# Attention units of a fused attention, ELU and SiLU kernel: normalising p by a diagonal product on TensorE

## The chip, the cores and the metric

One core of a Trainium2 chip runs the program. The metric is the device time of one execution in microseconds; before the change it is 877.9 us in the median of three runs (876.8 to 879.29).

## The reference

Causal attention with a window of 128 tokens and a linear bias for each head, over 4 sequences of 576 tokens, 8 heads of 64; then two pairs of dense layers, the first with an ELU, the second with a SiLU, on 2304 rows (512 to 2048 to 512 columns each).

```python
scores = scale * np.matmul(q, k.transpose(0, 1, 3, 2))
scores = np.where((rel >= 0) & (rel < 128), scores + bias[None], -1e9)
attn = np.exp(scores - np.max(scores, axis=-1, keepdims=True))
attn = attn / (np.sum(attn, axis=-1, keepdims=True) + 1e-09)
x = heads_to_columns(np.matmul(attn, v))          # 2304 x 512
h = x @ w_in; x = np.where(h > 0, h, np.exp(np.minimum(h, 0)) - 1) @ w_out
h = x @ w2_in; out = (h / (1 + np.exp(-h))) @ w2_out
```

The function that brings the heads into columns is written out in the reference. The weights come as 64-bit floats and are turned into 32-bit ones on the chip.

## The kernel before

**Attention** runs in 36 units. A unit is 256 query tokens of two heads (`UNITS`, L154): two blocks `e` of 128 tokens, two heads `j`. For each unit:

- `scores` (L460): 16 products on 64x64 parts of TensorE write two PSUM tiles `s0`, `s1`, one for each head (L470). VectorE adds the bias, takes the row minimum of the negated scores and writes p (L481); ScalarE takes the exponential in place and adds up the rows into `sm` (L489).
- `normal` (L496): VectorE adds 1e-9 to the four sums of a row and takes reciprocals (L501, L502: 128x4). GpSimd multiplies p by them row by row, four operations (L508).
- `turn` (L511): TensorE transposes p against an identity, 16 transposes of 64 columns (12 where a sequence begins, as in the first four units; L527), into the tile `t` of two banks. The index `x` (upper or lower 64 rows of p) picks the bank. VectorE copies head 0 (L537) and ScalarE head 1 (L539) to `pt` in SBUF, each from both banks.
- `mix` (L543), once for two units: p times v (L559), then to `xt` (L565).

There are three buffers of p and of pt. Two of the bias tables are made by GpSimd with a part masked at the sequence bounds, in `make_cuts` (L447): a copy of 128x1536 bf16 and a memset for each.

**Beside it** the weights are fetched and decoded: GpSimd scales the upper words (L331), ScalarE converts the lower (L333), VectorE joins them (L334, L336), and each weight is split into a high and a low part (L308, L311). The first 4 of 16 column groups of the first layer pair run during attention, block by block of 256 or 512 rows: `split_x` (L573, L574), `hidden` (L600; the ELU by L609, L585, L586, L612, L613) and `output_first` (L627). `make_ahead` forms combinations of blocks of x and stores them. **Then** `layers` runs the rest of both pairs (L927 for the input products, L1018 for the output products).

**The order of the work** is written by a planner (`Plan`, L35). Every piece is added with its engine, an assumed cost, the keys that it reads and writes, and for some a due time. `run` (L72) works backwards to a latest time for each, and then plays the engines forward: an engine that is free takes the ready piece with the earliest latest time. What comes out is each engine's fixed order; the waits on the chip come from the data. Loads go through the SP queue (one early load through ACT's) in the planner's order, over one modelled wire. The due time of a unit's scores is `unit_due` (L457): 4 us plus 3.2 us for each of the first 14 units, then 5.0.

Of the kernel before, what the change touches and what calls it, by code (L numbers as in the profile page):

```python
# [34 lines left out]
class Plan:  # L35
# [11 lines left out]
    def add(self, eng, cost, fn, r=(), w=(), due=1.0e9, moved=0, after=(), floor=0.0):  # L47
# [24 lines left out]
    def run(self):  # L72
        for op in reversed(self.ops):
            op.late = min([op.due] + [b.late - op.cost - self.between(op, b) for b in op.before])
        waiting = {op: len(op.after) for op in self.ops}
        ready = [(0.0, op) for op in self.ops if not op.after]
        queues, free = {}, {}
        for at, op in ready:
            queues.setdefault(op.eng, []).append((at, op))
        now, port = 0.0, 0.0  # L80
        left = len(self.ops)
        while left:
            ran = True
            while ran:
                ran = False
                for eng in queues:
                    if eng and free.get(eng, 0.0) > now:
                        continue
                    can = [x for x in queues[eng] if max(x[0], x[1].floor) <= now]
                    if not can:  # L90
                        continue
                    x = min(can, key=lambda x: (x[1].late, x[1].n))
# [12 lines left out]
                    left -= 1  # L105
                    ran = True
                    end = now + op.cost
                    free[eng] = end
                    if op.moved:
                        port = max(port, now + self.DMA_START) + op.moved / self.DMA_RATE  # L110
                        end = port
# [7 lines left out]
            times = [max(x[0], x[1].floor, free.get(e, 0.0) if e else 0.0) for e, q in queues.items() for x in q]  # L119
            if left:  # L120
                now = min(t for t in times if t > now)
        return max(op.end for op in self.ops)
# [3 lines left out]
def attention_elu_silu_kernel(  # L126
# [49 lines left out]
    UNIT, FAST, NFAST, START = 5.0, 3.2, 14, 4.0  # L176

# [222 lines left out]
    def start():  # L400
        load_q(0, nc.scalar, 1)
        load_k(0, n=1)
        add("DVE", 0.06, lambda: nc.vector.memset(T["warm",], 0.0), w=[("warm",)])
        add("ACT", 1.5, lambda: nc.scalar.activation(T["warm",], T["warm",], AF.Exp), w=[("warm",)], due=0.0)
        add("DVE", 0.27, lambda: nc.vector.memset(T["k", 0][:, :, P // 2:P], 0.0), w=[("kz",)], due=0.0)
        load_k(1, n=1)
        load_q(1, n=1)
        for i in range(3):
            add("DVE", 0.27, lambda i=i: nc.vector.memset(T["p", i][:, :, :, 0:PAD], 0.0), w=[("p", i, "lo")], due=0.1)
            add("DVE", 0.27, lambda i=i: nc.vector.memset(T["p", i][:, :, :, PAD + WIDE:], 0.0), w=[("p", i, "hi")], due=0.1)  # L410
# [12 lines left out]
        for x in range(2):  # L423
            add("POOL", 1.15, lambda x=x: relative(x), w=[("rel",)] + rk, due=0.0)
# [6 lines left out]
        for h in range(H):  # L431
            by = -(2.0 ** (-8.0 * (h + 1) / H)) / scale
            bf, bb = T["biasf",][:, h, P // 2:], T["bias",][:, h, :]
            if h < 2:
# [3 lines left out]
                    r=[("rel",)] + rk, w=[("bias", h)])  # L438
# [7 lines left out]

    def make_cuts():  # L447
        every = [("bias", h) for h in range(H)]

        def cut(name, rows, cols):  # L450
            nc.gpsimd.tensor_copy(T[name,], T["bias",])
            nc.gpsimd.memset(T[name,][rows, :, cols], MASKED / scale)
        add("POOL", 2.9, lambda: cut("biasm", slice(P // 2, P), slice(0, P)), r=every, w=[("biasm", h) for h in range(H)])
        add("POOL", 2.1, lambda: cut("biasa", slice(0, P // 2), slice(0, P // 2)), r=every, w=[("biasa", h) for h in range(H)])
# [5 lines left out]
    def scores(u):  # L460
        t, hp = UNITS[u]

        def products():
            for e in range(2):
                c0 = first_col(2 * t + e) // 2
                for x in range(2):
                    o = e * P + x * (P // 2)
                    for j in range(2):
                        rows = slice(j * D, (j + 1) * D)
                        nc.tensor.matmul(T["s", j][x * (P // 2):(x + 1) * (P // 2), e, c0:], T["q", t % 2][rows, hp, o:o + P // 2],  # L470
                                         T["k", t % 2][rows, hp, o + c0:o + WIDE], start=True, stop=True)
        tensor(0.74, products, r=[("q", t % 2, hp), ("k", t % 2, hp), ("kz",)], w=[("s", 0), ("s", 1)], due=unit_due(u))
        exps = []
        for j in range(2):
            for e in range(2):
# [4 lines left out]
                def biased(j=j, e=e, i=i, c0=c0, b=b):  # L480
                    nc.vector.tensor_tensor_reduce(  # L481
                        T["p", u % 3][:, j, e, PAD + c0:PAD + WIDE], T["s", j][:, e, c0:], T[b,][:, 2 * hp + j, c0:], -scale, 3.0e38,
                        ALU.add, ALU.min, T["neg", u % 4][:, i:i + 1])
                pk = [("p", u % 3, j, e)] + ([("p", u % 3, "lo"), ("p", u % 3, "hi")] if u < 3 else [])
                add("DVE", 0.29, biased, r=[("s", j), (b, 2 * hp + j)], w=pk[:1] + [("neg", u % 4, i)])
# [9 lines left out]

    def normal(u):  # L496
# [6 lines left out]
        add("DVE", 0.3, invert, w=sm)  # L503
        for j in range(2):
# [6 lines left out]
    def turn(u):  # L511
# [8 lines left out]
        def transposes():  # L520
            for j in range(2):
                for a, b2 in parts:
                    for i in range(a, b2):
                        e, c = i // 2, i % 2 * P + PAD
                        for x in range(2):
                            half = slice(x * (P // 2), (x + 1) * (P // 2))
                            nc.tensor.transpose(T["t",][:, x, j, i, :], T["p", u % 3][half, j, e, c - x * PAD:c - x * PAD + P],  # L527
                                                T["ident",][half, half])
        tensor(0.68, transposes, r=[("p", u % 3, j, e) for j in range(2) for e in range(2)]
               + [("p", u % 3, "lo"), ("p", u % 3, "hi"), ("ident",)], w=[("t", 0)], due=unit_due(u + 2) + 0.1)  # L530

        def evict(j):
            for a, b2 in parts:
                dst = T["pt", u % PTS][:, j, a * P:b2 * P].rearrange("p (i x q) -> p i x q", x=2, q=P // 2)
                src = T["t",][:, :, j, a:b2, :].rearrange("p x i q -> p x i q" if False else "p x i q -> p i x q")
                if j == 0:
# [3 lines left out]
        add("DVE", 0.61, lambda: evict(0), r=[("t", 0)], w=[("pt", u % PTS, 0)])  # L540
        add("ACT", 0.5, lambda: evict(1), r=[("t", 0)], w=[("pt", u % PTS, 1)])
# [42 lines left out]
    def elu(src, e):  # L584
        nc.vector.tensor_scalar(e, e, 1.0, -1.0, op0=ALU.min, op1=ALU.add)  # L585
        nc.vector.tensor_tensor(e, src, e, op=ALU.max)  # L586
# [3 lines left out]
    def hidden(bi, f, due):  # L590
# [19 lines left out]
        add("DVE", 0.16 + w * 1.55e-3, lambda: elu(T[m][:, 0:w], T[ek][:, 0:w]), r=[m], w=[ek])  # L610
# [271 lines left out]
    def activated(k, f, half, src, sk):  # L882
# [10 lines left out]
        elif slot("below", 2):  # L893
            def bent():
# [4 lines left out]
                r=[sk], w=[ek])  # L899
            add("ACT", 0.43, lambda: nc.scalar.activation(T[gk[0]], T[ek], AF.Copy), r=[ek], w=[gk[0]])  # L900
        else:
            add("ACT", 0.42, lambda: nc.scalar.activation(T[ek], src(), AF.Exp), r=[sk], w=[ek])
            add("DVE", 0.76, lambda: elu(src(), T[ek]), r=[sk], w=[ek])
# [3 lines left out]
    def quad(k, q, last):  # L907
# [30 lines left out]
        def sum_of(name, src):  # L938
            s, m = K[name], K[src]
            add("DVE", 0.475, lambda: nc.vector.tensor_tensor(T[s], T[m][:, 0:HALF], T[s], op=ALU.add), r=[m], w=[s])  # L940
# [38 lines left out]
    def outputs(k):  # L979
# [6 lines left out]
        for j in range(size):  # L986
            half = j // (size // 2)
            parts = 2 if k == len(steps) - 1 and j == size - 1 else 1
            for part in range(parts):
# [5 lines left out]
                def piece(fp, st=st, w=w, s=s, jj=jj, half=half):  # L995
# [35 lines left out]
                    else:  # L1031
                        add("DVE", 0.08 + w / 960.0, lambda: nc.vector.tensor_tensor(dst, T[m][:, 0:w], dst, op=ALU.add),  # L1032
                            r=[m], w=dk)
# [101 lines left out]
```

## Time and profile before

| | |
|---|---|
| median of three runs | 877.9 us |
| the profiled execution | 878.51 us |
| its span, first to last instruction | 876.7 us |
| TensorE busy | 858.5 us, 98% |
| VectorE, ScalarE, GpSimd busy | 603.1, 507.0, 136.2 us |
| mean granted TensorE clock | 0.994 |

The profile is taken in one execution. PE is TensorE, PEld its weight loads, DVE VectorE, ACT ScalarE, POOL GpSimd. Busy times are shares of the whole span, so a stage that is a twelfth of it hardly shows in them; it is read from tables of its own stretch. An engine's idle time is put down to the event that came last before it went on.

### The profile page before, as it was taken

The numbers are of one execution on the slowest core, as the hardware profiler recorded it, in microseconds if no ns is written. First come the engines' busy times: TensorE is split into PE (matmuls) and PEld (weight loads), VectorE is DVE, ScalarE is ACT, GpSimd is POOL, SyncE is SP. The second block draws the span as 40 slices with busy tenths as digits, with TensorE's granted clock in tenths as the row PEclk, the third lists the DMA queues.
The fourth block names the chain that finished last, engine by engine and source line by source line (L and its number), as shares of the span: only waits on it lengthen the run. The fifth ranks groups of instructions, "written<-read, shape, count | busy, mean of one in ns | idle before, by whom it ended". The sixth has DMA issues, their size and how long they took to land.

```text
span 876.7 us, 15017 instructions
## 1 busy us (share of the span) xinstructions
PE 858.5 (98%) x5520; PEld 772.8 (88%) x5520; DVE 603.1 (69%) x1385; ACT 507.0 (58%) x1191; POOL 136.2 (16%) x238
## 2 busy tenths in 40 slices
PE   6889999999999999999999999999999999999998
PEld 3667777778999999999999998989898989989997
DVE  6988989875997869796869878445746334633333
ACT  6979888865855556563657475656563334533331
POOL 8844434320110001110000220001100000100000
PEclk9979999999999999999999999999999999999999
DMA  9835686459460112280847345142236060226721
GB/s 308 290 116 189 206 270 212 156 188 369 186 243 1 37 55 90 76 322 1 322 170 286 146 150 222 63 189 73 97 113 259 0 252 25 73 73 220 261 97 72
DMA packets 67929, 142.00 MB, mean 162 GB/s; under 512 B 4368, under 2 KB 50192, under 8 KB 67856
## 3 DMA queue, kind: packets, MB, share of 16 engines
q1 hardware_dynamic: 67712, 140.92, 45.3%
q8 instruction: 43, 0.70, 0.3%
q14 instruction: 30, 0.25, 0.1%
q10 hardware_dynamic: 144, 0.13, 0.0%
HBM read 104.07 MB, written 36.96 MB: 161 GB/s over the span
## 4 chain that ended last, share of the span: by engine, by line
PE 89%; DVE 7%; ACT 2%; DMA 1%; issue 1%; POOL 0%; SPq 0%; POOLq 0%; DVEq 0%; ACTq 0%
PE m L1018 37%; PE m L927 33%; PE m L600 5%; PE m L627 5%; PE a L559 3%; PE s L470 3%; PE t L527 2%; DVE raw L334 1%; DVE p L481 1%; DVE raw L336 1%; DVE pt L537 1%; ACT p L489 1%; DVE w L311 1%; DVE g L905 0%; DMA q<-in_q_dram 0%
## 5 line engine op out<-in xcount | busy, mean ns | idle before, releaser
L1018 PE MATMUL m<-w,g 128*128 128x512 f32 (+1 forms) x876 | 211.9, 387 | 0.0
L1018 PEld LDWEIGHTS m<-w,g 128*128 128x128 f32 x876 | 161.6, 188 | 26.2
L1018 PE MATMUL m<-g,w 128*128 128x384 f32 x864 | 162.1, 336 | 0.7 <-DVE e L898 0.7
L1018 PEld LDWEIGHTS m<-g,w 128*128 128x128 f32 x864 | 151.6, 188 | 1.5 <-DVE e L898 1.2
L331 POOL TENSOR_SCALAR raw<-raw 128x512 f32<-128x512 f32 x60 | 47.5, 792 | 539.3 <-DMA raw<-in_moe_w_in_dram 258.3
L905 DVE TENSOR_TENSOR g<-e,g 128x384 fp32r<-128x384 f32 x168 | 93.9, 570 | 49.3 <-ACT e L891 43.1
L940 DVE TENSOR_TENSOR hs<-m,hs 128x384 f32<-128x384 f32 x84 | 46.7, 556 | 85.3 <-PE m L927 84.2
L927 PE MATMUL m<-c,wd 128*128 128x384 f32 x504 | 101.3, 335 | 0.0
L927 PE MATMUL m<-c,wc 128*128 128x384 f32 x504 | 101.2, 335 | 0.0
L927 PE MATMUL m<-c,wa 128*128 128x384 f32 x504 | 98.9, 336 | 0.0
L927 PEld LDWEIGHTS m<-c,wa 128*128 128x128 f32 x504 | 89.2, 188 | 2.6
L927 PEld LDWEIGHTS m<-c,wc 128*128 128x128 f32 x504 | 89.2, 188 | 2.1
L927 PEld LDWEIGHTS m<-c,wd 128*128 128x128 f32 x504 | 89.1, 188 | 2.0
L1032 DVE TENSOR_TENSOR acc<-m,acc 128x384 f32<-128x384 f32 (+2 forms) x85 | 51.4, 607 | 56.8 <-PE m L1018 56.6
L936 ACT ACTIVATE hs<-m 128x384 f32<-128x384 f32 x84 | 41.3, 491 | 84.3 <-PE m L927 83.8
L508 POOL TENSOR_SCALAR p<-p,sm 128x192 f32<-128x192 f32 (+1 forms) x144 | 74.5, 534 | 83.8 <-DVE sm L502 37.9
L489 ACT ACTIVATE p<-p,neg 128x192 f32<-128x192 f32 (+1 forms) x144 | 62.9, 441 | 7.6 <-DVE neg L481 6.6
L627 PE MATMUL m<-g,w 128*128 128x512 f32 (+1 forms) x240 | 57.2, 388 | 1.3 <-DVE e L586 0.7
L892 ACT ACTIVATE g<-hs 128x384 fp32r<-128x384 f32 x48 | 25.3, 527 | 57.2 <-DVE hs L940 56.9
L600 PE MATMUL m<-x,w 128*128 128x512 f32 (+1 forms) x240 | 55.3, 377 | 1.2 <-DVE x L574 1.2
L627 PEld LDWEIGHTS m<-g,w 128*128 128x128 f32 x240 | 42.9, 198 | 11.4 <-issue 1.3
L927 PE MATMUL m<-c,wb 128*128 128x384 f32 x252 | 50.7, 335 | 0.0
(124 smaller groups left out, 1189.2 us busy)
## 6 DMA issues: line engine op xcount, KB each, us to landing
c<-d SPq DMA_DIRECT2D x63, 768.0 KB, 6.6
raw<-in_moe_w_in_dram SPq DMA_DIRECT2D x32, 512.0 KB, 6.2
raw<-in_moe_w_out_dram SPq DMA_DIRECT2D x28, 512.0 KB, 3.6
d<-c SPq DMA_DIRECT2D x14, 768.0 KB, 4.6
d<-st SPq DMA_DIRECT2D x19, 384.0 KB, 3.1
k<-in_k_dram SPq DMA_DIRECT2D x16, 384.0 KB, 5.0
d<-xs SPq DMA_DIRECT2D x14, 384.0 KB, 3.0
v<-in_v_dram SPq DMA_DIRECT2D x18, 256.0 KB, 3.5
```

What stands on the lines that cost most here:

```text
L331: add("POOL", 0.66, lambda: nc.gpsimd.tensor_scalar(f32(top()), f32(top()), 2.0 ** -112, 1.0, op0=ALU.mult, op1=ALU.mult), w=top_k)
L470: nc.tensor.matmul(T["s", j][x * (P // 2):(x + 1) * (P // 2), e, c0:], T["q", t % 2][rows, hp, o:o + P // 2], T["k", t % 2][rows, hp, o + ...
L489: nc.scalar.activation(dst, dst, AF.Exp, bias=T["neg", u % 4][:, i:i + 1], scale=-1.0, accum_out=T["sm", u % 4][:, e, j:j + 1])
L508: nc.gpsimd.tensor_scalar(dst, dst, T["sm", u % 4][:, e, j:j + 1], 1.0, op0=ALU.mult, op1=ALU.mult)
L600: nc.tensor.matmul(T[m][:, 0:w], a[:, cs], T["x0", b2][:, c, 0:w], start=(c == 0 and x == 0), stop=(c == NKC - 1 and x == 2))
L627: nc.tensor.matmul(T[m][:, 0:w], a[:, cs], b2[:, 0:w], start=(f == 0 and x == 0), stop=(f == FIRST_F - 1 and x == 2))
L905: add("DVE", 0.475, lambda: nc.vector.tensor_tensor(T[gk[1]], T[ek], f32(T[gk[0]]), op=ALU.subtract), r=[ek, gk[0]], w=[gk[1]])
L927: nc.tensor.matmul(T[m][:, 0:HALF], a[:, cs], x[:, j, c, :], start=(begin and c == 0 and n == 0), stop=(c == 1 and n == 2), skip_group_che ...
L936: add("ACT", 0.4, lambda: nc.scalar.activation(T[s], T[m][:, 0:HALF], AF.Copy), r=[m], w=[s])
L940: add("DVE", 0.475, lambda: nc.vector.tensor_tensor(T[s], T[m][:, 0:HALF], T[s], op=ALU.add), r=[m], w=[s])
L1018: nc.tensor.matmul(T[m][:, 0:w], l, rr, start=(f == 0 and x == 0), stop=(f == n - 1 and x == 2))
L1032: add("DVE", 0.08 + w / 960.0, lambda: nc.vector.tensor_tensor(dst, T[m][:, 0:w], dst, op=ALU.add), r=[m], w=dk)
```

## The change

For units 0 to 11 (`DIAG = 12`) `normal` no longer has GpSimd scale p. VectorE multiplies a small stacked identity by the reciprocals and gets four diagonals of 64x64 per half (`diag`, one operation of 128x256), and `turn` multiplies p by them on TensorE instead of transposing it. From unit 12 on nothing of this changes. For all units the eviction is divided by bank (`x`) and not by head. The scores of units 1 and 3 go to the otherwise idle PSUM tiles `m1` and `m2`; scores are due 2 us earlier (`FEED`); six bf16 matmuls on zeros run at the start. The cut bias tables are copied by VectorE, two heads at a time. The planner gets a second resource, the port that VectorE and GpSimd share: pieces marked for it exclude each other in the plan. The ELU's two VectorE operations become two pieces of the plan.

```diff
 class Plan.add
+        op.port = eng in ("POOL", "DVE") if port is None else port
 Plan.run
-                    can = [x for x in queues[eng] if max(x[0], x[1].floor) <= now]
+                    can = [x for x in queues[eng] if max(x[0], x[1].floor) <= now and (port <= now or not x[1].port)]
...
+                    if op.port:
+                        port = end
...
+    SPARE = 1, 3
+    FEED, WARM, DIAG = 2.0, 6, 12
 start
+        zero = T["pt", PTS - 1].rearrange("p j t -> p (j t)").bitcast(BF16)[:, 0:5 * P]
+        def warm_up():
+            for _ in range(WARM):
+                nc.tensor.matmul(T["m", 0], zero[:, 0:P], zero[:, P:5 * P], start=True, stop=True)
+        add("DVE", 0.15, lambda: nc.vector.memset(zero, 0.0), w=[("pt", PTS - 1, 0)], due=0.0, port=False)
+        add("PE", 2.6, warm_up, r=[("pt", PTS - 1, 0)], w=[("m", 0)], due=0.0)
...
+                def second():
+                    for x in range(2):
+                        half = slice(x * (P // 2), (x + 1) * (P // 2))
+                        nc.vector.tensor_copy(ident2[half], T["ident",][half, half])
+                add("DVE", 0.25, second, r=[("ident",)], w=ident2_keys)
 make_cuts
-            nc.gpsimd.tensor_copy(T[name,], T["bias",])
-            nc.gpsimd.memset(T[name,][rows, :, cols], MASKED / scale)
+        for h in range(0, H, 2):
+                add("DVE", 0.2, lambda name=name, hs=hs: nc.vector.tensor_copy(T[name,][:, hs, :], T["bias",][:, hs, :]),
+                    r=[("bias", h), ("bias", h + 1)], w=keys)
+                add("POOL", cost, lambda name=name, hs=hs, rows=rows, cols=cols:
+                    nc.gpsimd.memset(T[name,][rows, hs, cols], MASKED / scale), w=keys)
 scores
+        sk = [("m", 1), ("m", 2)] if u in SPARE else [("s", 0), ("s", 1)]
-        tensor(0.74, products, r=[("q", t % 2, hp), ("k", t % 2, hp), ("kz",)], w=[("s", 0), ("s", 1)], due=unit_due(u))
+        tensor(0.74, products, r=[("q", t % 2, hp), ("k", t % 2, hp), ("kz",)], w=sk, due=unit_due(u) - FEED)
 normal
+    spot = acc[NBIG - 1]
+    diag = lambda u: spot[:, (8 + 2 * (u % 3)) * P:(10 + 2 * (u % 3)) * P].rearrange("p (i q) -> p i q", i=4)
+    ident2 = spot[:, 14 * P:14 * P + P // 2]
+        if u < DIAG:
+            add("DVE", 0.34, lambda: nc.vector.tensor_tensor(
+                diag(u), ident2.unsqueeze(1).to_broadcast([P, 4, P // 2]),
+                T["sm", u % 4].rearrange("p e j -> p (e j)").unsqueeze(2).to_broadcast([P, 4, P // 2]), op=ALU.mult),
+                r=sm + ident2_keys, w=diag_keys(u))
+            return
 turn
+                            if u < DIAG:
+                                nc.tensor.matmul(dst, src, diag(u)[half, 2 * e + j, :], start=True, stop=True)
+                            else:
+                                nc.tensor.transpose(dst, src, T["ident",][half, half])
...
-        def evict(j):
+        def evict(x):
-                dst = T["pt", u % PTS][:, j, a * P:b2 * P].rearrange("p (i x q) -> p i x q", x=2, q=P // 2)
+                dst = T["pt", u % PTS][:, :, a * P:b2 * P].rearrange("p j (i x q) -> p j i x q", x=2, q=P // 2)[:, :, :, x, :]
+                src = T["t",][:, x, :, a:b2, :]
-        add("ACT", 0.5, lambda: evict(1), r=[("t", 0)], w=[("pt", u % PTS, 1)])
+        add("ACT", 0.5, lambda: evict(1), r=[("t", 1)], w=[("pt", u % PTS, 1)])
 hidden
-        add("DVE", 0.16 + w * 1.55e-3, lambda: elu(T[m][:, 0:w], T[ek][:, 0:w]), r=[m], w=[ek])
+        add("DVE", 0.08 + w * 0.52e-3, lambda: clamp(T[ek][:, 0:w]), w=[ek])
+        add("DVE", 0.08 + w * 1.03e-3, lambda: nc.vector.tensor_tensor(T[ek][:, 0:w], T[m][:, 0:w], T[ek][:, 0:w], op=ALU.max),
+            r=[m], w=[ek], port=False)
```

Left out are `port=False` marks on pieces that read one operand from PSUM or write only, and the same division of the ELU in the later stage.

## Rows read from the trace of the kernel before

**Rows 1.** The page, busy time, share of the span and instructions of TensorE.

```profile
PE 858.5 (98%) x5520; PEld 772.8 (88%) x5520; DVE 603.1 (69%) x1385; ACT 507.0 (58%) x1191; POOL 136.2 (16%) x238
```

**Rows 2.** Busy time by stretch: us, engines (instructions), granted clock, DMA share, GB/s.

```profile
0.00:66.00 66.00, 52.21 (x598) 37.80 (x600) 53.47 (x201) 50.53 (x159) 44.84 (x93) 0.92 0.73 238
66.00:180.00 114.00, 113.83 (x1209) 85.35 (x1206) 98.95 (x342) 94.29 (x288) 47.48 (x91) 1.00 0.65 209
...
0.00:60.00 60.00, 46.46 (x518) 33.20 (x522) 48.53 (x178) 45.80 (x145) 43.06 (x89) 0.91 0.77 255
...
48.85:58.95 10.10, 9.34 (x56) 7.09 (x58) 9.84 (x30) 8.40 (x27) 3.66 (x7) 0.50 0.38 119
```

**Rows 3.** Waits from 0 to 60 us: us in total, times, longest.

```profile
PEld t L527 <- POOL p L508: 6.7, 9, 1.7
PE t L527 <- ACT pt L539: 5.0, 4, 1.5
DVE p L481 <- PE s L470: 4.5, 5, 1.6
...
DVE sm L501 <- ACT p L489: 2.3, 3, 1.0
...
PE s L470 <- DVE neg L481: 2.1, 3, 1.1
...
DVE pt L537 <- PE t L527: 1.4, 1, 1.4
...
PE t L527 <- POOL p L508: 0.3, 1, 0.3
...
PE t L527 <- DVE pt L537: 0.2, 1, 0.2
```

**Rows 4.** Timeline, both evictions of unit 0: start, us, instruction, idle before.

```profile
11.46 0.56 DVE L537 COPY pt<-t 128x384 f32<-128x384 f32 x1
...
12.05 0.49 ACT L539 ACTIVATE pt<-t 128x384 f32<-128x384 f32 x1 [0.49 <-DVE pt L537]
```

**Rows 5.** Timeline of TensorE, first scores and the stretch from 40 us.

```profile
3.74 1.34 PE L470 MATMUL s<-k,q 64*64 64x128 f32 x16 [3.74 <-DVE bias L437]
...
40.86 1.96 PE L559 MATMUL a<-pt,v 128*64 128x256 f32 x24
42.74 0.88 PE L470 MATMUL s<-k,q 64*64 64x192 f32 x16
43.56 0.72 PE L527 MATMUL t<-ident,p 64*128 64x64 f32 x16
44.20 1.70 PE L600 MATMUL m<-x,w 128*128 128x256 f32 x12
47.40 0.34 PE L527 MATMUL t<-ident,p 64*128 64x64 f32 x4 [1.50 <-ACT pt L539]
```

**Rows 6.** Line L501, 0 to 220 us: ns min/median/max.

```profile
L501 DVE TENSOR_SCALAR sm<-sm x36: 156/164/1135, 8.1 to 182.5; 128x4 f32<-128x4 f32 x36
```

**Rows 7.** Timeline, a POOL copy and VectorE beside it.

```profile
24.64 1.46 POOL L451 COPY biasa<-bias 128x1536 bf16<-128x1536 bf16 x1
...
24.99 1.14 DVE L501 TENSOR_SCALAR sm<-sm 128x4 f32<-128x4 f32 x1 [0.99 <-ACT p L489]
```

**Rows 8.** Groups of POOL, 0 to 60 us: busy us, mean ns, idle before.

```profile
L508 POOL TENSOR_SCALAR p<-p,sm 128x192 f32<-128x192 f32 (+1 forms) x47 | 23.5, 517 | 15.3 <-DVE sm L502 10.7 <-ACT acc L333 2.9 <-ACT w L308 1.5
L331 POOL TENSOR_SCALAR raw<-raw 128x512 f32<-128x512 f32 x8 | 5.6, 706 | 0.0
...
L451 POOL COPY biasm<-bias 128x1536 bf16<-128x1536 bf16 x1 | 1.5, 1469 | 0.0
```

**Rows 9.** Groups of VectorE by shape, 0 to 60 us.

```profile
L501 DVE TENSOR_SCALAR sm<-sm 128x4 f32<-128x4 f32 x12 | 3.6, 303 | 2.3 <-ACT p L489 2.3
...
L574 DVE TENSOR_TENSOR x<-xt,x 128x256 fp32r<-128x256 f32 x4 | 2.4, 600 | 0.0
...
L613 DVE TENSOR_TENSOR g<-e,g 128x256 fp32r<-128x256 f32 x2 | 1.3, 660 | 0.0
L585 DVE TENSOR_SCALAR ex<-ex 128x256 f32<-128x256 f32 x2 | 1.1, 562 | 0.0
L586 DVE TENSOR_TENSOR e<-m,e 128x256 f32<-128x256 f32 x2 | 0.8, 424 | 0.1
...
L585 DVE TENSOR_SCALAR e<-e 128x256 f32<-128x256 f32 x2 | 0.6, 284 | 0.0
```

**Rows 10.** The one-input operation on 512 elements, 0 to 220 us.

```profile
L585 DVE TENSOR_SCALAR e<-e 128x512 f32<-128x512 f32 x10 | 4.2, 417 | 2.8 <-ACT e L609 2.5
```

More of the change, by code (lines that the diff above doesn't have):

```diff
@@ L45, in __init__, with add @@
         self.ops, self.writer, self.readers = [], {}, {}
-    def add(self, eng, cost, fn, r=(), w=(), due=1.0e9, moved=0, after=(), floor=0.0):
+    def add(self, eng, cost, fn, r=(), w=(), due=1.0e9, moved=0, after=(), floor=0.0, port=None):
         op = Op(eng, cost, fn, due, moved and self.DMA_START + moved / self.DMA_RATE or self.DRAIN.get(eng, 0.0), len(self.ops))
         op.moved, op.floor = moved, floor
+        op.port = eng in ("POOL", "DVE") if port is None else port
         op.after.update(after)
@@ L79, in run @@
             queues.setdefault(op.eng, []).append((at, op))
-        now, port = 0.0, 0.0
+        now, wire, port = 0.0, 0.0, 0.0
         left = len(self.ops)
@@ L108, in run @@
                     free[eng] = end
+                    if op.port:
+                        port = end
                     if op.moved:
-                        port = max(port, now + self.DMA_START) + op.moved / self.DMA_RATE
-                        end = port
+                        wire = max(wire, now + self.DMA_START) + op.moved / self.DMA_RATE
+                        end = wire
                     op.end = end
@@ L118, in run @@
                     break
-            times = [max(x[0], x[1].floor, free.get(e, 0.0) if e else 0.0) for e, q in queues.items() for x in q]
+            times = [max(x[0], x[1].floor, free.get(e, 0.0) if e else 0.0, port if x[1].port else 0.0)
+                     for e, q in queues.items() for x in q]
             if left:
-                now = min(t for t in times if t > now)
+                now = min([t for t in times if t > now] or [now + 0.05])
         return max(op.end for op in self.ops)
@@ L423, in start @@
         for x in range(2):
-            add("POOL", 1.15, lambda x=x: relative(x), w=[("rel",)] + rk, due=0.0)
+            add("POOL", 1.15, lambda x=x: relative(x), w=[("rel",)] + rk, due=0.0, port=False)
         def relative_first():
@@ L437, in start @@
                 add("DVE", 0.27, lambda bb=bb, by=by: nc.vector.tensor_scalar(bb, rel, by, None, op0=ALU.mult),
-                    r=[("rel",)] + rk, w=[("bias", h)])
+                    r=[("rel",)] + rk, w=[("bias", h)], port=False)
             else:
@@ L539, in evict @@
                     nc.scalar.activation(dst, src, AF.Copy)
-        add("DVE", 0.61, lambda: evict(0), r=[("t", 0)], w=[("pt", u % PTS, 0)])
-        add("ACT", 0.5, lambda: evict(1), r=[("t", 0)], w=[("pt", u % PTS, 1)])
+        add("DVE", 0.61, lambda: evict(0), r=[("t", 0)], w=[("pt", u % PTS, 0)], port=False)
+        add("ACT", 0.5, lambda: evict(1), r=[("t", 1)], w=[("pt", u % PTS, 1)])
     def mix(u):
@@ L582, in store_x, with clamp @@
              NKC * w * P * 4, r=[("xt", bi % 2, c, o // w) for c in range(NKC)], w=[("xd", b, t)])
[L584 removed]
+    def clamp(e):
         nc.vector.tensor_scalar(e, e, 1.0, -1.0, op0=ALU.min, op1=ALU.add)
[L586 removed]
     e0_n = [0]
@@ L902, in activated @@
             add("ACT", 0.42, lambda: nc.scalar.activation(T[ek], src(), AF.Exp), r=[sk], w=[ek])
-            add("DVE", 0.76, lambda: elu(src(), T[ek]), r=[sk], w=[ek])
+            add("DVE", 0.28, lambda: clamp(T[ek]), w=[ek])
+            add("DVE", 0.475, lambda: nc.vector.tensor_tensor(T[ek], src(), T[ek], op=ALU.max), r=[sk], w=[ek], port=sk[0] != "m")
             add("ACT", 0.43, lambda: nc.scalar.activation(T[gk[0]], T[ek], AF.Copy), r=[ek], w=[gk[0]])
@@ L939, in sum_of @@
             s, m = K[name], K[src]
-            add("DVE", 0.475, lambda: nc.vector.tensor_tensor(T[s], T[m][:, 0:HALF], T[s], op=ALU.add), r=[m], w=[s])
+            add("DVE", 0.475, lambda: nc.vector.tensor_tensor(T[s], T[m][:, 0:HALF], T[s], op=ALU.add), r=[m], w=[s],
+                port=False)
         def active(name, fi, half):
@@ L1032, in piece @@
                         add("DVE", 0.08 + w / 960.0, lambda: nc.vector.tensor_tensor(dst, T[m][:, 0:w], dst, op=ALU.add),
-                            r=[m], w=dk)
+                            r=[m], w=dk, port=False)
                     if layer == 1 and sw == len(SWEEPS[1]) - 1:
```

37 lines of the change are left out of this document (19 added, 18 removed).

## The prediction

> **What bounds the kernel now.** I read the busy shares first: TensorE (PE) is busy for 858.5 of 876.7 us [rows 1], so only 18.2 us of idle time are left in the whole run, and the question is where they lie. The table by stretches answers it [rows 2]: 13.8 us lie in the first 66 us (66 less 52.21), while from 66 to 180 us PE idles for 0.17 us of 114. A second loss stands in the same table. From 48.85 to 58.95 us the granted clock is 0.50, the 1.2 GHz level, while PE is busy for 9.34 us; at 2.4 GHz that work needs 4.7 us less. So what this change can win lies ahead of 66 us, where attention units, the splitting of the weights and the first block share the engines; after that PE runs without gaps, and a microsecond won earlier stays won.
>
> In the first 60 us VectorE (DVE) is busy for 48.53 us, TensorE for 46.46 [rows 2]: the two hold each other up. The waits of that stretch say how [rows 3]. PE waits 5.0 us for ACT's eviction of the transposed p in four waits; its weight loads wait 6.7 us in nine for GpSimd's (POOL's) scaled p. These are largely the same holes. PE waits 2.1 us for DVE to leave the score banks. DVE in turn waits 4.5 us for scores, 2.3 us for exponentials and 1.4 us for transposes. The evictions run one behind the other: DVE's copy starts at 11.46 and takes 0.56 us, ACT's starts at 12.05 [rows 4]. The hole ahead of 47.40 us, 1.50 us wide, is such a wait [rows 5], and the clock is down soon after it.
>
> Last, what POOL does to DVE: POOL's copy of 1.46 us starts at 24.64 us, and an operation on 128x4 elements that has a median of 164 ns [rows 6] sits on DVE from 24.99 for 1.14 us, until the copy ends [rows 7].
>
> **The change part by part.**
>
> *Removed from POOL.* For units 0 to 11 the row scaling goes: 47 such operations took 23.5 us in the first 60 us [rows 8] (the 48th starts behind them). Both copies for the cut bias tables, 1.5 us each, go to DVE. POOL keeps the weights' scaling, 0.706 us each. POOL is not the bound, so its time counts at nothing; what counts is that its step leaves the way from sums to transposes and that it blocks DVE less. The blocked time in four groups of rows is: 12 x (303 - 164 ns) = 1.7 us for L501; 2 x (562 - 284) = 0.6 for L585; against the 424 ns of another two-input operation on 128x256, 4 x (600 - 424) = 0.7 for L574 and 2 x (660 - 424) = 0.5 for L613 [rows 6, 9]. Together 3.4 us; as POOL's weight scaling stays, I take 3.0. Ends: 1.0, about the share in which scaling and copies are not at fault, and 3.4.
>
> *Added to DVE.* Twelve products of 128x256 for the diagonals: 424 ns each by the nearest row in size and kind [rows 9], 5.1 us; 284 ns, a one-input operation of that size, is the low end (3.4), L574's disturbed 600 ns the high one (7.2). Eight copies of 128x384 in bf16: the one-input rows give 284 ns for 256 and 417 ns for 512 four-byte elements [rows 9, 10], so 0.52 ns an element over some 0.15 us; 384 two-byte elements counted as 192 give 0.25 us, together 2.0, with 0.15 and 0.35 us each as ends (1.2 and 2.8). Two small copies of the identity at 164 ns and the memset for the warm-up at 284 ns come to 0.6. Sum 7.7 us, ends 5.2 and 10.6. Net of the blocked time DVE gets 4.7 us more. Part of it fits where DVE waits today: with the score banks of units 1 and 3 spare, and transposes that no longer wait for POOL, I give back 2.0 of its 4.5 us for scores (the first score tile stays late) and the 1.4 us for transposes [rows 3]. That leaves **+1.3 us** by which DVE is later; with ends of -1.6 (5.2 less 3.4 of blocking and 3.4 of filled waits) and +8.2 (10.6 less 1.0 and 1.4). The copies of the identity wait for POOL's mask, and the first diagonal for them; the operations behind them on DVE queue with them, as they queue behind the score tiles now. The diagonals lie in a part of the output accumulator that the first reload of x for the combinations overwrites; that reload waits for the store of units 8 to 11 anyway, so it is late by nothing.
>
> *Waits of PE removed.* Eviction by bank lets DVE and ACT read side by side: each of the four eviction waits loses about one DVE copy, 0.6 us [rows 4], 2.4 of 5.0 us; the rest is DVE coming late, and stays. The waits on POOL (0.3) and on DVE's copy (0.2) go as well [rows 3]. Scores in spare banks, with due times 2 us earlier, take 1.9 of 2.1 us. Together **-4.8 us**; ends 0 (all come back as waits on DVE) and -7.6 (all of 5.0 + 0.2 + 0.3 + 2.1).
>
> *Clock.* If the holes of this size go, the stretch at 0.50 goes with them: 4.7 us at most. DVE is busy for 9.84 of its 10.10 us [rows 2], so about half would have been a wait for DVE: **-2.4 us**, ends 0 and -4.7. The six warm-up matmuls run while PE waits for the first loads, ahead of 3.74 us [rows 5]: nothing, unless they run past that, when the first scores queue behind them.
>
> *Added to PE.* 176 transposes (48 in the first four units, 128 in the other eight) become products in f32. Sixteen transposes took 0.64 us from start to start (43.56 to 44.20), 40 ns each; sixteen score products 0.82 us, 51 ns each [rows 5]. The product against a diagonal has the moving columns of the transpose and the arithmetic of the scores; I take 51 ns: 176 x 11 ns = 1.9 us. Half falls into PE's remaining idle time, **+1.0 us**. The ends are 0 (as transposes) and the mixes: 24 in 1.88 us, 78 ns each [rows 5], 6.7 us in all.
>
> The Trainium skill (FP8 and Floating Point Precision, TensorE Precision Notes) says that a true FP32 product goes through the array four times. The mixes move 8 x 256 + 16 x 128 = 4096 f32 columns in two halves of the array in those 1.88 us; four passes at 2.4 GHz would be 3.4 us, so this trace does not show them. By the page each new product would be 107 ns, an estimate, and this step 11.8 us if no two ran side by side, a sum of 884 us.
>
> *The plan.* Splitting the elu into two entries, and letting only operations marked for the port exclude each other, changes order and no work: nothing, because PE's order is unbroken from 66 us on. If that cover is broken, each late entry costs what PE then waits; the bound is the 4.4 us of idle that PE has after 66 us today, in either direction.
>
> **Sum**: -4.8 - 2.4 + 1.3 + 1.0 = -4.9 us. The profiled execution took 878.5 us (span 876.7), which gives 873.6; the median of the runs shown, 877.9, lies 0.6 lower, so I predict 873.0 us.
>
> **The rivals.**
>
> *A. DVE alone sets the pace.* Then only DVE's account counts: +7.7 - 3.0, less the three waits at most (2.9 + 1.4 + 1.5), and the half-clock stretch returns elsewhere, since PE still has long gaps. That is -1 us: 877. For it: DVE is over 90% busy through the clock stretch. Against: 11.5 us of DVE's first 60 are idle. The Trainium skill (TensorE: Matmul & The Clock Gate, Part 1) says that half rate is the default and that only activity lifts it; by this rule a faster but still patchy start could be slow again, and the row at 0.50 behind a hole agrees. It also holds if the evictions still queue behind each other, the change not doing what it says.
>
> *B. The start closes up.* PE loses all 7.6 us of the waits and the whole 4.7, and pays 1.9 for products: 878.5 - 10.4 = 868.1, 867.5 against the median. For it: both parties to the waits are relieved at once. Against: somebody must still do 4.7 us more on DVE.
>
> *C. Slower: DVE becomes the later one.* The diagonal stands on DVE between the sums and the products, and behind each the unit's copy. At its high price (7.2 us) with high copies, and only 1.0 us of blocking returned, DVE gains 9.6 us; less 2.4 us of filled waits (scores 1.0, transposes 1.4), 7 us; PE's waits at the transposes go (-2.9) and the clock stays: 878.5 + 4, say 882. It decides when a diagonal takes over about 0.6 us on the path. For it: DVE is 97% busy in the stretch of the low clock [rows 2]; against: the two-input rows of the same size at 424 ns.
>
> *D. Products priced as the mixes.* With 78 ns each PE gets 6.7 us instead of 1.0 on its way through the first stage, and the time is 879, no change. For it: both are f32 products on full columns; against: most of a mix's 78 ns goes with its two to four times as many columns.
>
> **How the numbers follow.** This kernel's runs tell 0.3% (2.6 us) from no change. The forecast has 0.48 (its own range is 870 to 875.6), B 0.14, A 0.22, C 0.11, D 0.05. Faster, below 875.3: B and all but 0.02 of the forecast, 0.60. Slower, above 880.5: C, and 0.05 of A, where the broken cover of the plan's order costs its 4.4 us: 0.16. Same: the other 0.17 of A, D and 0.02 of the forecast, 0.24. The range leaves out the fast half of B, most of C and the slow end of A, together just under 0.2: 866 to 881.
>
> **What would show each step.** The clock at 1.00 through the first 66 us, against a new stretch at 0.50. ACT's eviction starting with DVE's, not behind it. No L508 row for twelve units, DVE's 128x4 operation near 164 ns. The diagonal's own row: 0.42 us right, over 0.6 case C. Sixteen products from start to start: 0.8 us right, 1.25 case D. PE's idle time ahead of 66 us: 13.8 now, 8 to 9 as forecast, under 6 in B. The forecast falls if PE's new waits in the first 60 us name DVE with more than 8 us, or if holes appear behind 66 us.

## The result, and the profile after

The changed kernel takes 885.4 us in the median of six runs (883.8 to 887.6), the kernel before in the same series 877.7: 1.0091 times, 95% interval 1.0072 to 1.0109. It is slower by 7.7 us, and the forecast, 873.0 with a range to 881, was wrong in sign. The profiled execution is one of the two slowest of the six (887.63 us; its mean granted clock, 0.990, is the lowest, with 0.992 to 0.996 in the others), so differences read from its page are some 2 us larger than those of the medians.

The page of the changed kernel: busy time, share, instructions, and the clock in 40 slices.

```profile
PE 875.4 (99%) x5702; PEld 785.6 (89%) x5702; DVE 607.0 (69%) x1408; ACT 506.5 (57%) x1191; POOL 111.4 (13%) x194
...
PEclk7899999999999999999999999999999999999999
```

Against [rows 1], TensorE's idle time falls from 18.2 to 10.4 us, by 7.8, and its busy time rises from 858.5 to 875.4, by 16.9. The difference of 9.1 us is that of the two spans. Both figures hold the six warm-up matmuls, 2.7 us of work put where TensorE was idle before:

```profile
1.25 2.74 PE L418 MATMUL m<-pt 128*128 128x512 bf16 x6 [1.25 <-DVE warm L409]
```

Without them 5.1 us of idle time are gone, and the work that came is over seven times the 1.9 us that the prediction priced.

The table by stretches (columns as in [rows 2]):

```profile
0.00:66.00 66.00, 59.05 (x688) 46.01 (x690) 50.61 (x203) 46.03 (x148) 16.61 (x46) 0.87 0.73 236
66.00:180.00 114.00, 113.63 (x1189) 82.05 (x1188) 96.94 (x337) 92.12 (x282) 49.18 (x86) 1.00 0.63 201
10.00:26.00 16.00, 13.63 (x116) 11.12 (x118) 8.54 (x40) 7.50 (x28) 5.24 (x12) 0.50 1.07 369
```

Ahead of 66 us PE idles for 6.95 us instead of 13.8, while VectorE does 2.9 us less than before in the same time: the pace there has passed to TensorE. A stretch at 0.50 lies from 10 to some 27 us. In the place of the old one, from 48.85 us, the clock is now full:

```profile
48.85:58.95 10.10, 9.61 (x128) 8.27 (x125) 8.71 (x27) 7.25 (x20) 1.13 (x4) 1.00 0.60 185
```

But the start of the kernel before was slow too, which its rows do not say. First the kernel before, its transposes at two times and the clock of that stretch, then the first scores of the changed kernel:

```profile
10.51 0.90 PE L527 MATMUL t<-ident,p 64*128 64x64 f32 x12
21.64 0.59 PE L527 MATMUL t<-ident,p 64*128 64x64 f32 x12 [0.83 <-ACT pt L539]
10.00:20.00 10.00, 8.47 (x97) 5.19 (x93) 6.96 (x35) 7.02 (x27) 9.58 (x19) 1.00 1.08 361
...
3.93 1.34 PE L494 MATMUL s<-k,q 64*64 64x128 f32 x16
8.01 0.77 PE L494 MATMUL s<-k,q 64*64 64x128 f32 x16 [1.43 <-DMA q<-in_q_dram]
```

The same twelve transposes take 0.90 us at 10.51 and 0.59 at 21.64, with the clock given as 1.00 from the start up to 48.85. By such durations TensorE works at the lower level up to some 18 us in the kernel before, and up to 7 us in the changed one, which falls back to it at 10.

TensorE in order of time in the changed kernel, to be read against [rows 5]:

```profile
11.48 2.82 PE L565 MATMUL t<-acc,p 64*128 64x64 f32 x24
15.49 2.82 PE L565 MATMUL t<-acc,p 64*128 64x64 f32 x24 [1.18 <-ACT pt L578]
...
40.62 1.86 PEld L565 LDWEIGHTS t<-acc,p 64*128 64x128 f32 x32
40.62 2.00 PE L565 MATMUL t<-acc,p 64*128 64x64 f32 x32
42.55 0.62 PE L638 MATMUL m<-x,w 128*128 128x256 f32 x3
43.10 0.88 PE L494 MATMUL s<-k,q 64*64 64x192 f32 x16
```

The line of the products and its weight loads, all twelve units (ns min/median/max):

```profile
L565 PEld LDWEIGHTS t<-acc,p x352: 182/188/330, 11.5 to 71.2; 64*128 64x128 f32 x176
L565 PE MATMUL t<-acc,p x352: 272/272/471, 11.5 to 71.2; 64*128 64x64 f32 x176
```

Sixteen products hold TensorE from 40.62 to 42.55 us, 1.93 us, where sixteen transposes took 0.64: 1.29 us more for a unit at the high clock. The 176 products of the program leave 352 records, two each; the 544 transposes of before leave 544. The first three units of twelve products fall into the stretch at 0.50 and take about 2.8 us each. (A record is one instruction as the trace counts it.) The bands of 16 and 24 records under scores and mixes are no different: the loop that issues the scores of one unit (L460; cut to its heads) makes eight products,

```python
for e in range(2):
    for x in range(2):
        for j in range(2):
            nc.tensor.matmul(T["s", j] ...
```

and the trace shows sixteen, which are the "16 products" in the description of the kernel before. Each of these plain f32 products is two records, each transpose one. The prediction divided both by the number of records.

The evictions of the first two units, DVE's line L576 and ACT's L578, and the waits among them to 66 us (us in total, times, longest):

```profile
14.36 0.56 DVE L576 COPY pt<-t 128x384 f32<-128x384 f32 x1 [1.88 <-PE t L565]
14.95 0.49 ACT L578 ACTIVATE pt<-t 128x384 f32<-128x384 f32 x1 [3.92 <-DVE pt L576]
...
18.36 0.49 ACT L578 ACTIVATE pt<-t 128x384 f32<-128x384 f32 x1 [2.11 <-PE t L565]
18.89 0.56 DVE L576 COPY pt<-t 128x384 f32<-128x384 f32 x1 [2.53 <-ACT pt L578]
```

```profile
ACT pt L578 <- DVE pt L576: 7.2, 4, 3.9
...
DVE pt L576 <- ACT pt L578: 4.6, 4, 2.5
...
PE t L565 <- ACT pt L578: 1.8, 2, 1.2
...
PE t L565 <- DVE pt L576: 1.2, 1, 1.2
...
PE s L494 <- DVE neg L505: 0.8, 2, 0.4
```

They still follow each other, in all 36 units, now with either engine first. The change does not do here what it says.

VectorE's groups to 66 us, against [rows 9]:

```profile
L535 DVE TENSOR_TENSOR acc<-acc,sm 128x256 f32<-128x256 f32 x11 | 4.6, 422 | 0.2
...
L531 DVE TENSOR_SCALAR sm<-sm 128x4 f32<-128x4 f32 x11 | 2.7, 242 | 0.3 <-ACT p L513 0.3
...
L613 DVE TENSOR_TENSOR x<-xt,x 128x256 fp32r<-128x256 f32 x4 | 1.7, 420 | 0.0
...
L472 DVE COPY biasm<-bias 128x384 bf16<-128x384 bf16 x4 | 1.2, 306 | 0.0
...
L653 DVE TENSOR_TENSOR g<-e,g 128x256 fp32r<-128x256 f32 x2 | 0.8, 420 | 0.0
...
L624 DVE TENSOR_SCALAR ex<-ex 128x256 f32<-128x256 f32 x2 | 0.6, 288 | 0.0
```

This account came out: a diagonal takes 422 ns (424 forecast), the disturbed rows fell to 242 and 420 ns.

### The profile page after: what moved, and what is told of

It reads as the page before. It is cut to its first block, busy times and chain, and to the rows that moved or that the text cites. A ratio compares the mean times of both kernels' runs of the same rounds, so it can differ in the third digit from the quotient of the medians.

```text
span 885.8 us, 15339 instructions
## 1 busy us (share of the span) xinstructions
PE 875.4 (99%) x5702; PEld 785.6 (89%) x5702; DVE 607.0 (69%) x1408; ACT 506.5 (57%) x1191; POOL 111.4 (13%) x194
## 4 chain that ended last, share of the span: by engine, by line
PE 97%; DVE 1%; DMA 1%; ACT 0%; SPq 0%; issue 0%; DVEq 0%
PE m L1060 39%; PE m L968 35%; PE m L638 6%; PE m L667 6%; PE a L598 4%; PE s L494 3%; PE t L565 3%; PE t L567 2%; DMA q<-in_q_dram 1%; DVE pt L576 0%; DMA v<-in_v_dram 0%; ACT pt L578 0%; DVE acc L342 0%; DVE p L505 0%; SPq L390 0%
## 5 line engine op out<-in xcount | busy, mean ns | idle before, releaser
L1060 PEld LDWEIGHTS m<-g,w 128*128 128x128 f32 x864 | 151.7, 188 | 0.3 <-DVE e L938 0.2
L337 POOL TENSOR_SCALAR raw<-raw 128x512 f32<-128x512 f32 x60 | 45.1, 752 | 551.0 <-DMA raw<-in_moe_w_in_dram 220.5
L544 POOL TENSOR_SCALAR p<-p,sm 128x192 f32<-128x192 f32 x96 | 55.2, 591 | 78.8 <-DVE sm L532 48.2
L638 PE MATMUL m<-x,w 128*128 128x512 f32 (+1 forms) x240 | 58.6, 383 | 0.0
L638 PEld LDWEIGHTS m<-x,w 128*128 128x128 f32 x240 | 40.4, 188 | 11.8 <-issue 4.6
L667 PEld LDWEIGHTS m<-g,w 128*128 128x128 f32 x240 | 40.5, 188 | 11.5 <-issue 3.4
```

The source lines that it names most:

```text
L337: add("POOL", 0.66, lambda: nc.gpsimd.tensor_scalar(f32(top()), f32(top()), 2.0 ** -112, 1.0, op0=ALU.mult, op1=ALU.mult), w=top_k)
L544: nc.gpsimd.tensor_scalar(dst, dst, T["sm", u % 4][:, e, j:j + 1], 1.0, op0=ALU.mult, op1=ALU.mult)
L638: nc.tensor.matmul(T[m][:, 0:w], a[:, cs], T["x0", b2][:, c, 0:w], start=(c == 0 and x == 0), stop=(c == NKC - 1 and x == 2))
L667: nc.tensor.matmul(T[m][:, 0:w], a[:, cs], b2[:, 0:w], start=(f == 0 and x == 0), stop=(f == FIRST_F - 1 and x == 2))
L1060: nc.tensor.matmul(T[m][:, 0:w], l, rr, start=(f == 0 and x == 0), stop=(f == n - 1 and x == 2))
```

## The experiments

All times are medians beside runs of the kernel before on the same chip (877.7 to 878.3 us in the four series); brackets hold the ratio to it with its interval. The theory: the products are dear on TensorE. The rivals: VectorE's added work, the new order (above all the port in the plan), the clock.

**e1, transposes in place of products.** Everything else as in the changed kernel; the first twelve units are not normalised.

```diff
-                            if u < DIAG:
-                                nc.tensor.matmul(dst, src, diag(u)[half, 2 * e + j, :], start=True, stop=True)
-                            else:
-                                nc.tensor.transpose(dst, src, T["ident",][half, half])
+                            nc.tensor.transpose(dst, src, T["ident",][half, half])
```

> The changed kernel with its plan, its order and its diagonals on VectorE, but TensorE transposes p against the identity in the first twelve units instead of multiplying by the diagonal (this leaves the normalisation of those units out). Theory 1 (the products cost too much on TensorE: 1.93 us for sixteen against 0.64 us of transposes, 12 units, some 15.5 us and more at the low clock): PE's busy time falls by 15 us or more, the time to 869 to 874 us. Rival 2 (VectorE's added work or the new order is what costs): PE's idle time takes up what its busy time loses, the time stays above 881 us.

877.3 us (0.9993, 0.9983 to 1.0003), 8.0 below the changed kernel; PE's busy time falls by 14.4 us, to 861.0. The theory holds, its size does not: 4.1 us of the 14.4 come back as PE's idle time (875.5 less 861.0 is 14.5, against 10.4), and the 10.3 us left are 8.0 between the medians. Take the products out and the change is worth nothing. Some of PE's waits of this run up to 66 us, without the products' work between them:

```profile
PE t L564 <- ACT pt L575: 3.9, 2, 2.1
...
PE t L564 <- DVE pt L573: 2.0, 2, 1.2
...
PE s L494 <- DVE neg L505: 0.2, 1, 0.2
```

The waits on the score banks have gone; those on the evictions, 5.9 us, are no shorter than the 5.2 of the kernel before.

**e2, no diagonals; e7, nor the port in the plan.**

```diff
-    FEED, WARM, DIAG = 2.0, 6, 12
+    FEED, WARM, DIAG = 2.0, 6, 0
 e7 also
-        op.port = eng in ("POOL", "DVE") if port is None else port
+        op.port = False
```

> The changed kernel with no unit on the diagonal way (GpSimd scales p in all 36 units as before); everything else of the change stays, and the plan is worked out anew. Theory 1: 870 to 876 us, PE busy near 858 us. Rival 2 (the port in the plan, the spare banks or the earlier due times give a worse order): 881 us or more even without the products.

> As e2 (no unit on the diagonal way), and the plan does not know the shared port (no piece is marked), so that it plans VectorE and GpSimd as free of each other, as before. If the port's rule in the plan is what makes e2 3.7 us slower than the kernel before, this run gives 876 to 879 us; if the spare banks, the earlier due times, the cuts or the warm-up do it, 881 us or more.

e2: 881.6 us (1.0046, 1.0031 to 1.0061), as its rival had it. e7: 877.8 (1.0003, 0.9992 to 1.0015). So a second part of the loss is the port's rule in the plan, some 4 us. e2 by stretches, then its order of time at one place:

```profile
0.00:60.00 60.00, 46.17 (x528) 32.39 (x528) 46.03 (x186) 45.13 (x145) 40.26 (x87) 0.86 0.80 258
16.00:36.00 20.00, 15.14 (x120) 10.46 (x120) 12.70 (x42) 11.71 (x36) 13.75 (x25) 0.60 0.97 335
```

```profile
27.09 2.50 PE L638 MATMUL m<-x,w 128*128 128x256 f32 x10 [0.68 <-DVE w L317]
29.53 0.90 PE L567 MATMUL t<-ident,p 64*128 64x64 f32 x12
30.47 0.56 DVE L576 COPY pt<-t 128x384 f32<-128x384 f32 x1 [2.61 <-PE t L567]
```

VectorE is busy for 46.03 us of the first 60, against 53.45 in e7 with the same operations to do. At 27 us ten matmuls of the first block stand ahead of the transposes that VectorE and ScalarE wait for, at the half clock. It is the order that is worse; which of the plan's decisions led there was not tried.

**e3, pt laid out by bank; e5, and two PSUM tiles.** What the two evictions write no longer interleaves; e5 also splits the tile `t`.

```diff
-        fixed(att_p, ("pt", i), [P, 2, 4 * P], F32)
+        fixed(att_p, ("pt", i), [P, 2, 2, 4, P // 2], F32)
 evict
+                dst = T["pt", u % PTS][:, x, :, a:b2, :]
 mix
-                                         ptt[:, j, a * P:b2 * P], start=(i == 0 and x == 0),
+                                         ptt[:, :, j, a:b2, :].rearrange("p x i q -> p i x q"), start=(i == 0 and x == 0),
 e5 also
-    fixed(ps_p, ("t",), [P, 2, 2, 4, P // 2], F32)
+    for x in range(2):
+        fixed(ps_p, ("t", x), [P, 2, 4, P // 2], F32)
```

> The changed kernel with pt laid out by bank, so that the two evictions of a unit write separate stretches and not interleaved ones; order and plan are the same. Theory: they follow each other in all 36 units now only because what they write interleaves; then they overlap here (by about 0.5 us in most units), PE's waits for evictions in the first 60 us (3.0 us) shrink by half and the time falls by 1 to 3 us. Rival: they are kept apart by the tile they read, and nothing changes (within 1 us).

> The changed kernel with pt laid out by bank (as in e3) and the transposed p in two PSUM tiles of one bank each instead of one tile of two. In e3 the evictions still never overlapped, so what keeps them apart is not the stretch that they write. Theory: it is the shared tile t; with two tiles they overlap in most of the 36 units, and PE's waits for evictions (3.0 us) halve: 882 to 884.5 us. Rival: the fixed order of the engines keeps them apart in time anyway, no overlaps, 884 to 886 us.

e3: 884.8 us (1.0080, 1.0064 to 1.0096), no pair of evictions overlaps; its theory fell. e5: 881.8 (1.0041, 1.0026 to 1.0057), and 34 of 36 pairs overlap. Two units of e5 in order of time:

```profile
14.51 0.56 DVE L577 COPY pt<-t 128x384 f32<-128x384 f32 x1 [1.91 <-PE t L566]
14.55 0.49 ACT L579 ACTIVATE pt<-t 128x384 f32<-128x384 f32 x1 [3.41 <-PE t L566]
...
18.04 0.56 DVE L577 COPY pt<-t 128x384 f32<-128x384 f32 x1 [1.32 <-PE t L566]
18.09 0.49 ACT L579 ACTIVATE pt<-t 128x384 f32<-128x384 f32 x1 [1.84 <-PE t L566]
```

So the shared PSUM tile kept them in series, although the halves lie in different banks. Whether two tiles would do with the interleaved pt was not run.

**e6, the kernel before with the mended eviction alone.** The edits of e5 and eviction by `x`, nothing else of the change.

> The kernel before with eviction by bank alone, done as in e5 (two PSUM tiles, pt by bank). If the two evictions of a unit run side by side, PE's waits for ACT's eviction (5.0 us) lose about one copy each: 874 to 876.5 us. If VectorE and ScalarE come late for other reasons, 877 to 879 us, no change.

876.0 us (0.9974, 0.9964 to 0.9984), 33 of 36 pairs overlap. It is the fastest complete version, by 2.3 us against the kernel before and by 9 to 10 against the changed one; of the others only e10 lies below the kernel before.

**e4, the kernel before with the diagonals alone** (`second`, `diag`, the products and their cost in the plan, as in the change).

> The kernel before with the diagonal way for the first twelve units alone (second identity, diagonals, products); no other part of the change. Theory 1: PE's busy time rises by some 15 us; of this 5 to 8 us fall into idle time, the time is 883 to 891 us. Rival 2 (the products alone are covered, another part costs): within 3 us of the kernel before.

887.4 us (1.0120, 1.0093 to 1.0146); PE's busy time rises by 14.3 us, to 872.8. The diagonal way alone, in the old order, costs at least as much as the whole change (the intervals overlap).

**e8, no warm-up.**

```diff
-        add("PE", 2.6, warm_up, r=[("pt", PTS - 1, 0)], w=[("m", 0)], due=0.0)
```

> The changed kernel without the six warm-up matmuls. In the changed kernel the granted clock is 0.50 from about 10 to 26 us, while the products of the first units run. Theory: the burst raises the clock for the first scores only and the patchy stage behind it loses it again, so without the burst the time is the same within 1.5 us. Rival: the burst is worth its place, without it 2 us or more slower.

884.7 us (1.0075, 1.0047 to 1.0102): the same. Its table shows 1.00 for the clock in every stretch, and yet:

```profile
13.92 2.82 PE L564 MATMUL t<-acc,p 64*128 64x64 f32 x24
...
24.92 1.65 PE L564 MATMUL t<-acc,p 64*128 64x64 f32 x24
```

The same 24 records take 2.82 us, and later 1.65. Where no change of the clock is on record yet, its row says nothing; the duration of a known piece does.

**e9, the whole change without the port in the plan.** The second edit of e7 alone.

> The changed kernel with all twelve units on the diagonal way, and no shared port in the plan. The port's rule cost 3.9 us without diagonals (e2 881.6 against e7 877.8). Theory: it costs the same with them, 880.5 to 883 us. Rival: with GpSimd nearly idle in the first 60 us the rule has little left to forbid, so that it costs under 1.5 us here: 884 to 886 us.

881.2 us (1.0044, 1.0024 to 1.0063): 4.2 us below the changed kernel, though GpSimd has little to do. The rival fell.

Step by step from e7, which takes the time of the kernel before: the port's rule adds 3.9 us (e2) and the diagonal way another 3.7 (the changed kernel), together the loss. Of these 3.7 the products are 8.0 (e1); the rest of the diagonal way, GpSimd's scaling gone, gives back 4.3 (e2 less e1). The price of the diagonal way hangs on the order around it: 3.4 us without the rule (e7 to e9), 9.5 in the old plan (e4).

**e10, e11, e12, e15: the rule out and the evictions mended**, with no diagonals, with diagonals but transposes for products, with diagonals in four units, and with all twelve.

```diff
 all four: the edits of e5, and
+        op.port = False
 e10  DIAG = 0    e11  DIAG = 12, transposes as in e1    e12  DIAG = 4    e15  DIAG = 12
```

> As e7 (no diagonals, no port in the plan) with the evictions mended as in e5 (two PSUM tiles, pt by bank). The mended evictions gave 2.3 us over the kernel before (e6) and 3.6 over the changed one (e5). Theory: they add to e7's 877.8, so 874 to 876 us. Rival: spare banks, cuts on VectorE and earlier scores use up the same waits and give nothing with them, so no better than e6's 876.0.

> As e9 with the evictions mended as in e5, and transposes in place of the products (the normalisation of the first twelve units is left out): the diagonal way at the price of PE that the prediction was near. Theory that the rest of the prediction's sum holds once its pieces are there: 871 to 875 us. Rival A of the prediction (VectorE alone sets the pace): 876 to 878 us, with PE's waits in the first 60 us named after VectorE.

> As e10 with the first four units on the diagonal way (48 products, some 5 us more for PE, in a stretch where PE is idle for 8 to 9 us of 20). Theory: there PE has the room, and the freed GpSimd brings the weights earlier: 872 to 875 us, better than e10. Rival: the first units sit on the way to the first mix, so that their longer products count in full: 877 us or more.

> As e11 but with the products: no port in the plan, evictions mended, twelve units on the diagonal way, complete. Against e11 (875.5) it prices the products alone where nothing else is amiss. Theory: PE's busy time rises by 14 to 16 us; part of it takes up idle time, 878 to 882 us. Rival: the idle time covers them, under 877 us.

e10: 877.3 us (0.9986, 0.9976 to 0.9995). e11: 875.5 (0.9972, 0.9962 to 0.9982). e12: 879.1 (1.0024, 0.9998 to 1.0050). e15: 883.1 (1.0058, 1.0039 to 1.0077). The theories of e10, e12 and e15 missed; e11 came out between its theory and rival A. The products alone cost 7.6 us (e15 less e11), with 10.3 us more of busy time for PE (869.7 against 859.4); in the four first units alone they already cost at least what they free. e10 is not better than e6: the earlier scores, spare banks and VectorE's cuts give nothing on top of the mended evictions. Nor do the mended evictions always pay: e15 runs the plan of e9 and e10 that of e7, and neither is clearly faster than it (their intervals overlap), while e5 gained 3.6 us and e6 2.3. Why was not tried. In e11 PE waits, up to 60 us, for

```profile
PE t L565 <- DVE pt L574: 3.0, 3, 2.0
PE m L665 <- DVE ex L647: 2.7, 1, 2.7
```

that is for VectorE, as rival A said, though the time is half a microsecond below its range.

**e13, products in halves of 64 stationary columns; e16, the same in e15.**

```diff
+                                for y in range(2):
+                                    ys = slice(y * (P // 2), (y + 1) * (P // 2))
+                                    nc.tensor.matmul(dst[ys], src[:, ys], diag(u)[half, 2 * e + j, :], start=True, stop=True)
```

> The changed kernel with each product made as two on 64 stationary columns each (64x64 parts, as the scores are), order and plan the same. The trace of the changed kernel shows two matmuls and two weight loads of 188 ns for each product of 128 stationary columns, 60 ns from one to the next; the scores with 64 columns have one of each, 51 ns. Theory: the doubling comes with 128 f32 stationary columns, so the halves stay 32 matmuls for 16 products, at 40 to 51 ns: 1.3 to 1.65 us in place of 1.93 for a unit, the time 881 to 884 us. Rival: every f32 product with a diagonal doubles, 64 matmuls, 890 us or more.

> As e15 with the products in halves of 64 columns, as in e13. Theory: 2 to 4 us below e15, and at best at the level of the kernel before with mended evictions (e6, 876.0). Rival: no better than e15.

e13: 880.9 us (1.0030, 1.0018 to 1.0043). e16: 878.7 (1.0010, 0.9999 to 1.0020). Each is about 4.5 us faster than with whole products. e13 in order of time, and its line:

```profile
38.02 1.16 PE L567 MATMUL t<-acc,p 64*64 64x64 f32 x64
39.11 0.62 PE L640 MATMUL m<-x,w 128*128 128x256 f32 x3
```

```profile
L567 PE MATMUL t<-acc,p x395: 218/218/365, 30.0 to 64.8; 64*64 64x64 f32 x198
L567 PEld LDWEIGHTS t<-acc,p x394: 129/135/223, 30.0 to 64.8; 64*64 64x64 f32 x197
```

The theory of this run fell: the halves double as well, 64 records for sixteen products. But a unit takes 1.09 us, not 1.93. The two halves together have the columns of the whole; both kinds of record became shorter, the weight load 135 ns against 188 and the matmul 218 against 272, and parts of 64x64 stand in the place of parts of 64x128. The weight loads (PEld) are busy for 1.86 us of each whole unit and for 1.02 of a halved one, nearly all of it both times. That they are what holds the products back is likely from this, but no run parts the shorter loads from the smaller parts of the array.

**e14, the measured cost in the plan.**

```diff
-        tensor(0.68 + 0.3 * (u < DIAG), transposes, ...
+        tensor(0.68 + 1.25 * (u < DIAG), transposes, ...
```

> The changed kernel with the products' measured cost in the plan (0.68 + 1.25 us and not 0.68 + 0.3). Theory: the order hardly matters next to the work, which is the same, 883 to 887 us. Rival: the plan's wrong price makes the order bad, with the right one 880 us or less.

884.1 us (1.0063, 1.0046 to 1.0080), as the theory had it: the work, not its price in the plan.

## Why the prediction was wrong, point by point

**Added to PE**, the step that failed: "Sixteen transposes took 0.64 us from start to start (43.56 to 44.20), 40 ns each; sixteen score products 0.82 us, 51 ns each". They were eight products, each with two records, 102 ns apiece; the mixes' 24 were twelve, 157 ns apiece. Read so, the same rows [rows 5] would have given 176 x 62 ns = 10.9 us by the scores and 20.6 us by the mixes, where the prediction had 1.9 and 6.7. Measured: 121 ns a product at the high clock, 14.4 us of busy time (e1), of which 8.0 us are lost time (7.6 with the rest mended, e15 against e11), where the forecast had +1.0. That about half would fall into idle time came out.

**The rule of the page** was set aside by the same slip. The mixes move 4 x 256 + 8 x 128 = 2048 columns, not 4096; in two halves of the array that work side by side four passes at 2.4 GHz are 1.71 us of the 1.88 measured. So this trace agrees with the Trainium skill (FP8 and Floating Point Precision, TensorE Precision Notes) that true FP32 takes four passes, and the text should have carried that price. By that rule, an estimate, a new product is 53 ns with the two halves of rows side by side and 107 without. That the text's 107 and the sum of 884 us lie near the measured 121 ns and 885.4 us is partly luck, for the plan's 4 us and the shares of idle time are not in them.

**The plan**, put down as nothing "because PE's order is unbroken from 66 us on", cost about 4 us (e2 against e7, e9 against the changed kernel). What counts is the order ahead of 66 us, where PE waits.

**Waits of PE removed**: -4.8 forecast. The fall of idle time by 7.8 us is no measure of it, for 2.7 are the warm-up, and where the products stand PE has more to do while it would wait. The waits on evictions fell from 5.2 to 3.0, on score banks from 2.1 to 0.8; with transposes in place of the products (e1) they are 5.9 and 0.2. So the spare banks and the earlier scores gave the 1.9 us forecast, and the eviction by bank gave nothing: the evictions did not overlap. That they might not was a clause of rival A; with two tiles they do, worth 2.3 us to the kernel before (e6).

**Clock**: -2.4 forecast. The stretch that the forecast meant has gone, as it said, and one from 10 to 27 us has come. With the slow starts that the rows leave out, the work at the lower level is some 20 us in the kernel before (11 up to 18 us, and 9.3) and some 17 in the changed one (2.7 for the first scores, and 14.7), the warm-up left out: an estimate from the durations and stretches of these two executions. Half of the difference would be the gain, 1 to 2 us; no run measures it alone. Why the clock fell at 10 us was not tried; without the warm-up the time is the same (e8).

**Added to VectorE**: right. Its busy time rose by 3.9 us (607.0 against 603.1), 4.7 net were forecast. Diagonals 422 ns each, copies 306 and 273 ns (250 forecast). Of the blocking 2.5 us came back (3.0 forecast): 0.7 from L531, 0.7 from L613, 0.5 and 0.6 from the other two groups.

**The rivals.** C named the sign and the wrong engine: with cheap products VectorE does not make the kernel slower (e1, e11). A, 877 us, is what the change gives once the products are taken out (e1, 877.3), and e11 shows VectorE as the one waited for. D named the right place, with a price taken from the same miscounted rows.

## What to carry to other kernels

Before a row is divided by its count, the count is held against the instructions that the program issues: here each f32 product is two records and each transpose one, so moving a scaling into "the transpose that is done anyway" tripled its time on the engine that bounds the kernel. Relieving an engine with time to spare (GpSimd) at the bounding one's cost has to be paid by waits that really vanish: here 4.3 us came back for 8.0. Two engines read two banks side by side only if nothing else ties them: here it took two tiles.

## What the runs showed of the hardware

An f32 product of 64 moving columns on 64 rows takes 121 ns with 128 stationary columns and 68 ns as two halves of 64 stationary columns (1.09 us for sixteen), with twice as many records; an f32 transpose of the first shape takes 40 ns. The granted clock reads 1.00 up to its first recorded change, also where the same twelve transposes take 0.90 us instead of 0.59 (the kernel before), or the same 24 records 2.82 instead of 1.65 (e8).
